# Rebuilding w_r and w_v in the score banks of the second batch's first head, with VectorE making the low halves

## The chip, the cores and the metric

The kernel runs on one core of a Trainium2 chip. The metric is the device time of one execution in microseconds (us). The core has five queues of work that matter here: TensorE (PE, the matmuls, with its weight loads PEld), VectorE (DVE), ScalarE (ACT), GpSimd (POOL) and SyncE (SP, which issues every DMA). PSUM is the accumulator memory that TensorE writes; SBUF is the working memory.

## What is computed

Two stages follow one another: an attention whose queries are pooled in pairs, and a channel mix ("ff" below) over the attention's output.

```python
q_pool = q.reshape(B, H, S // 2, 2, D).mean(axis=3)      # B 8, H 8, S 1152, D 64
scores = scale * q_pool @ k^T;  attn = softmax(scores);  x = attn @ v     # x: (8, 576, 512)
xk = mu_k * x + (1 - mu_k) * x_prev;  xr = mu_r * x + (1 - mu_r) * x_prev
k = relu(xk @ w_k)                 # w_k 512 x 1024
v = (k * k) @ w_v                  # w_v 1024 x 512
out = sigmoid(xr @ w_r) * v        # w_r 512 x 512
```

Inputs and output are float32. The kernel splits each float32 factor into a 16-bit high half and a 16-bit low half and adds three products (high by high, high by low, low by high). The weights are split once, at the start.

## The kernel before

**Attention.** The 64 heads (n = 0 to 63, eight to a batch) are worked on in turn, and each head's 576 pooled queries in six blocks of 96 (`block`). A block i has one of three score slots in PSUM, `s_b[i % 3]`, two banks wide. Its chain is: nine matmuls of scores (L530), the row maximum on VectorE (L537), a transpose of it (L540), a second maximum (L544), a matmul that spreads it (L546), a copy on ScalarE into the queries' low half (L550), nine more matmuls (L556), and the exponential on ScalarE (L562), which empties the slot. GpSimd makes the low half of the result (L565). `window` then multiplies with v (L591, L593, L598) into the bank `a_b`, and a head's result goes into `xt`, of which there are three, one for each batch in turn.

**Channel mix.** `ff` works on tiles of 256 rows of x. For each tile it mixes neighbouring rows (L734, L737, L743, L745), does the k product in four pairs of f through the PSUM bank `f_b` (matmuls L765; relu L792, square L794, low half L796), and then, for two halves of 128 rows, the r product, four ScalarE operations, a gate on VectorE (L820), the v product and a last VectorE product (L829). A tile becomes possible when its batch's attention is done; batch 0 holds tiles 0 and 1 whole. The tile loop stands at the end of each batch (L861 and after).

**Weights.** `weights` splits one block of 128 x 512 of a weight matrix at a time: w_k has 8 blocks, w_r 4 and w_v 8. The raw 64-bit pairs come by DMA (512 KB a block) into one of four staging buffers, `st[0]`, `st[1]` and two that lie in `xt[2]`. ScalarE turns the high words into `f_b` in PSUM (L680) and the top bytes in place (L684). VectorE joins both into `ex` in SBUF (L687, mode 'W1'). ScalarE writes the 16-bit high half (L697), and GpSimd subtracts it to give the low half (L702). All 20 blocks are placed beside the attention of batch 0, w_k first. One GpSimd memset (L844) then gives `xt[2]` back for batch 2.

**Order.** Every operation is put on a list with what it reads and writes (`Issue.add`). The order of issue on each of the five queues is a stored, compressed list (`TURNS`); engines issue in that order, and the dependences are kept by semaphores. While the order is laid out, `gaps` puts filler matmuls on zeros (L871) into TensorE's pauses of the first 150 us of its own planned time.

Of the kernel before, what the change touches and what calls it, by code (L numbers as in the profile page):

```python
# [12 lines left out]
F32 = mybir.dt.float32  # L13
# [6 lines left out]
ALU = mybir.AluOpType  # L20
# [30 lines left out]
    "c-n<}349e*miMW8Rqxf?>+Nfjm*i#N6S6_rx3C3}2!s|42!gVyAVdX31-DU*+S1zMzBS|Yw4<QyXe)F(-D=~~O4C7H={U9ss3^h@mplJ+E1>gz{r"  # L51
    "$dk->bTH_vQT0a;r$S>7-?Hh!l!bB4Z;}Rg>XhBpeFHqAHO;9`}d+L_WXQOD2)aYr1?cM4V(eoJ6`onwNCHk2Ewvq#2q=bJ$J0#~suh4$W?aOe3m"
    "!b-U)EsNH7hDL<*Y+oq|y8rMQ0P19qVrn+ouI2<Ln!*F;a4#lqMZi?6gcE3I1uxnZ*?1*TT@601j*EA!NMHSVE@I%rQ(fpc9N;ubHcpZ*7DhE(IW"
    "Ot<O_ITKZLd6ueId!|PC!8tLRGU*R$mhDgU<^-c+(%BA(;4$76HdiYVq`cCXUy=#?J<YlTSO5(pX?5g-5x_Fw^ooJvpdkVk96H;i+Q=Y;fciKhU!"
    "!8d3lC2L=J~L?9jb-okAH|H5IdCWwe4=hU=0ys@uq>dLp^GR&CVHSM8Bp!U}L*!mPtCtJkDGVMo6d&CAp6eqE3998i~QV)}8_p?d8U=9=URp&wmC"
    "MXZ~y5$`YdRBnz%HVvDcN+VE766vvmSS+3si{++9q|+%R+mgv-G#XFDYogJpZ6F~Wixq^!;oNWp!4^V0VUqE1ZOHEr_(5hQ;`dW9m>&#LFyJ-4UY"
    "|GO^@Y5Xy+}0!6fjNG?e@9d<i_8HrvRCT&oB%;Iow9TZ#c=}$LjdK<n>^=9GVUua@a{Pp#1!Te6r=)K$Of$CR1vHC_hX2nf!EKG8|4*2o#TnqEQN"
    "llax#(6BIX1J)-4>qrOns=kt+26!S&nQHn-9YDjgtOqa{!^|@Vcx9aqh&*x7oU~~^U)D7KXklpTbdo_>8>(LCCtIg$V)tpXE)9jv<$CK16HJ8gBa"
    "h14T0heJQo%zG<8XI%bXt0#SFvwvCr-KUZnfy$q8l%mqYObng)09dTq?Ek8++51Z$<0Zm6CjGm^WsG5N=i|Z64_)T9*<KDDXB;rD`skDG^#aGgV$"
    "!OBeS|w^_!TNN15n$Fp(V~bYqatjt(b=U>NO2d&6qOsM8!?4AA8=oJa)gG#bXa7&2Db?J~F^#+nZvve~i1Xvshzdz*d8e7jw>%Q+O}gS{Qoa`O<>"  # L60
    "9A+!5aVC+IYfGnd5HM!2OjM0TBWY60LkTLLOtE+@PFf@~GQv!vVYFIAYxIPu-aX4texFZOeIC{AaJjJBAmwbGTuu%~voXn-;4}tdn1F*e!jKa(ii"
    "}Gz{^fGPF(datBGL-Zq><B!IZWhfj6=H^t4*!0tgfoAvR76(=9JH>D6de<kX%d^w(|0d(lRP7Ei5c7D$EvTsj!TcOjAi|F)7(BRTYqyHzftiNwot"
    "afK`qyJ#5%QN<~wu8jsJ36DAo`6bds_0|=Tw6ozaIXeKkg2NVu@JONL=S!*s2n1Lm{m1a!lFfIZnbDvKIWK>TO)A1WL4i7%B$L&VDgAKpmi8*3!`"
    "C6_4e#y(3gfKx%BPo%{<Rx-)hURo5V_r^94%t$%WPS{k1DGdMNi~^J)mV(8!C*KTgltzL#OST73+o|mdN3IB1<=3l4ay-0%n>|nKabn%33|+Wb8W"
    "3mC;xK4iJ^vFAQQXi$NqUd5HR4jPA5>K>n?H{F^EtjG};I*I-jMf;q}U$$!4*@g@sNdKfj{@fabKE{QUgI`T3N|3|)}PP+p#zo109glSu$2oo3D="
# [222 lines left out]
def kernel(  # L288
# [221 lines left out]
    def block(n, j, i, t):  # L510
# [337 lines left out]
    for n in range(B * H):  # L848
# [63 lines left out]
```

## Time and profile before

| | |
|---|---|
| median of 3 runs | 1111.04 us (1110.21 to 1111.13) |
| the profiled execution, whole | 1111.68 us |
| its span, first to last instruction | 1109.9 us |
| TensorE busy | 1084.1 us (98%) |
| TensorE weight loads busy | 896.5 us (81%) |
| VectorE busy | 882.0 us (79%) |
| ScalarE busy | 842.0 us (76%) |
| GpSimd busy | 805.3 us (73%) |
| DMA moved | 135.38 MB |

The profile's page gives the busy time of each engine; the view by windows gives the same for any stretch; the view by groups gives the mean duration of each kind of instruction. A matmul's duration in these views is from its start to the end of its last result, and matmuls overlap in the array, so that a stretch can show TensorE "busy" though it does less than it could. How much it does is counted from the number of matmuls and the distance between their starts.

### The profile page before, as it was taken

Reading aid. Unit: us, or ns where it says so; the run is one execution under the profiler, and the core shown is the slowest. Engines: PE = TensorE matmul, PEld = TensorE weight load, DVE = VectorE, ACT = ScalarE, POOL = GpSimd, SP = SyncE. Lnnn points to the kernel's source line nnn. Section 1 sums busy time; section 2 is a strip of 40 time slices with the busy share of each in tenths; the row PEclk is TensorE's granted clock in tenths of the full one; section 3 lists DMA queues with packets and bytes.
Section 4 is the critical chain, followed back from the end, with each engine's and each line's share of the span. In section 5 each row is a group of like instructions: output and inputs, shape, how many; then the busy total and the mean of one; then the engine's idle time right before and its main releaser. Section 6 shows DMA issues by size and latency. Waiting matters only on the chain.

```text
span 1109.9 us, 45181 instructions
## 1 busy us (share of the span) xinstructions
PE 1084.1 (98%) x19046; PEld 896.5 (81%) x19046; DVE 882.0 (79%) x1587; ACT 842.0 (76%) x1804; POOL 805.3 (73%) x940
## 2 busy tenths in 40 slices
PE   7888999999999999999999999999999999999998
PEld 7777888988788897988797888888797979787564
DVE  7888888899898888888787888787888889773321
ACT  6899987877777786877877777878777778765643
POOL 4778978877768786878777786868688768755431
PEclk9999999999999999999999999999999999999999
DMA  9989557766567755656555565556556365420000
GB/s 246 220 220 221 136 123 147 144 152 108 135 125 133 148 108 104 142 131 129 135 94 128 122 126 113 124 135 110 128 111 150 83 129 100 88 40 23 19 20 29
DMA packets 258155, 135.38 MB, mean 122 GB/s; under 512 B 193440, under 2 KB 230304, under 8 KB 257952
## 3 DMA queue, kind: packets, MB, share of 16 engines
q1 hardware_dynamic: 257952, 132.50, 55.5%
q8 instruction: 149, 2.44, 0.9%
q14 instruction: 54, 0.44, 0.1%
HBM read 67.11 MB, written 9.44 MB: 69 GB/s over the span
## 4 chain that ended last, share of the span: by engine, by line
PE 70%; DVE 1%; issue 0%; ACT 0%; DVEq 0%
PE f L765 28%; PE s L556 9%; PE s L530 9%; PE a L591 5%; PE a L593 5%; PE a L598 4%; PE s L765 4%; PE a L765 2%; PE s L540 1%; PE s L546 1%; DVE mx L537 0%; DVE xr L737 0%; DVE xk L737 0%; DVE qn L435 0%; DVE mb L544 0%
## 5 line engine op out<-in xcount | busy, mean ns | idle before, releaser
L537 DVE TENSOR_REDUCE mx<-s 128x96 f16<-128x864 f32 x384 | 399.9, 1053 | 85.5 <-PE s L530 42.3
L565 POOL TENSOR_SCALAR pl<-pf 128x864 f16<-128x864 uint16 (+1 forms) x384 | 333.5, 869 | 143.6 <-ACT pf L562 108.9
L562 ACT ACTIVATE pf<-s 128x864 int32<-128x864 f32 x384 | 335.0, 885 | 89.6 <-PE s L556 64.8
L591 PE MATMUL a<-vt,pf 128*128 128x65 f16 x2880 | 238.7, 193 | 0.7 <-DVE xb L622 0.4
L593 PE MATMUL a<-vt,pf 128*128 128x64 f16 x2880 | 239.1, 193 | 0.0
L530 PE MATMUL s<-qT,ks 128*128 128x96 f16 x3456 | 221.4, 206 | 6.0 <-ACT pf L562 4.6
L556 PE MATMUL s<-qT,ks 128*128 128x96 f16 x3456 | 214.3, 206 | 4.2 <-ACT qT L550 3.9
L591 PEld LDWEIGHTS <-pf 128*128 128x128 f16 x2880 | 202.4, 98 | 5.1
L530 PEld LDWEIGHTS <-ks 128*128 128x128 f16 x3456 | 181.7, 98 | 29.1 <-issue 8.0
L593 PEld LDWEIGHTS <-pf 128*128 128x128 f16 x2880 | 193.1, 97 | 8.4 <-issue 1.2
L556 PEld LDWEIGHTS <-ks 128*128 128x128 f16 x3456 | 178.6, 98 | 24.3 <-issue 4.5
L550 ACT ACTIVATE qT<-s 1x96 f16<-1x96 f32 x384 | 88.2, 233 | 77.7 <-PE s L546 70.1
L544 DVE TENSOR_REDUCE mb<-s 128x1 f16<-128x128 f32 x384 | 108.9, 287 | 40.9 <-PE s L540 33.5
L765 PE MATMUL f<-xlk,wk_hi 128*128 128x256 f16 x496 | 135.2, 272 | 0.1
L765 PE MATMUL f<-xhk,wk_hi 128*128 128x256 f16 x496 | 135.1, 272 | 0.0
L765 PE MATMUL f<-xhk,wk_lo 128*128 128x256 f16 x496 | 135.2, 273 | 0.0
L598 PE MATMUL a<-vb,pl 128*128 128x65 f16 x2304 | 126.6, 193 | 0.4 <-POOL pl L565 0.2
L765 PEld LDWEIGHTS <-wk_hi 128*128 128x128 f16 x1152 | 105.6, 98 | 14.4
L598 PEld LDWEIGHTS <-pl 128*128 128x128 f16 x2304 | 101.0, 98 | 6.9 <-POOL pl L565 0.4
L796 POOL TENSOR_TENSOR gl<-g 128x512 f16<-128x512 f32 x72 | 76.9, 1069 | 40.5 <-ACT g L794 37.0
L478 POOL TENSOR_TENSOR kn<-kr,kn 128x320 f16<-128x320 f32 (+1 forms) x126 | 97.0, 784 | 6.0 <-ACT kn L473 1.8
L765 PE MATMUL f<-wv_lo,g 128*128 128x512 f16 x240 | 90.9, 379 | 0.0
(114 smaller groups left out, 2174.1 us busy)
## 6 DMA issues: line engine op xcount, KB each, us to landing
kr<-in_k_dram SPq DMA_DIRECT2D x64, 288.0 KB, 3.3
vr<-in_v_dram SPq DMA_DIRECT2D x64, 288.0 KB, 3.3
qr<-in_q_dram SPq DMA_DIRECT2D x32, 320.0 KB, 3.6
ks<-ks SPq DMA_DIRECT2D x64, 144.0 KB, 2.7
out_dram<-em SPq DMA_DIRECT2D x36, 256.0 KB, 2.3
qr<-in_q_dram SPq DMA_DIRECT2D x32, 256.0 KB, 3.3
st<-in_moe_w_k_dram SPq DMA_DIRECT2D x4, 512.0 KB, 5.5
xt<-in_moe_w_k_dram SPq DMA_DIRECT2D x4, 512.0 KB, 6.5
```

The source lines that it names most:

```text
L478: lambda cs=cs, en=nc.vector if ve else nc.gpsimd: en.tensor_tensor(kn[i][:, cs, D:P], kr[i][:, cs], kn[i][:, cs, 0:D], op=ALU.subtract),
L530: nc.tensor.matmul(cols(c, c + 1), ks1[hp][:, c, :], qhi, start=(c == c0), stop=False, skip_group_check=True)
L537: op("DVE", 0.974, lambda: nc.vector.tensor_reduce(mxz[:, P - QN:P], grid(0, NC).rearrange("p c q -> p q c"), axis=AX.X, op=ALU.max), r=[( ...
L544: op("DVE", 0.199, lambda: nc.vector.tensor_reduce(mbz, s[:, 0:P], axis=AX.X, op=ALU.max), r=[("s", z)], w=[("mb", z)], key=t + O_MAX)
L550: op("ACT", 0.15, lambda: nc.scalar.activation(qlo[0:1], s[0:1, 0:QN], AF.Prelu, scale=1.0 - EPS, alpha=(1.0 + EPS) / (1.0 - EPS)), r=[("s ...
L556: nc.tensor.matmul(cols(c, c + 1), ks2[hp][:, c, :], qlo, start=False, stop=True, skip_group_check=True)
L562: op("ACT", NC * QN / 1200 + 0.051, lambda: nc.scalar.activation(pf[:, :, HALF + rows.start:HALF + rows.stop], grid(0, NC), AF.Exp, bias=S ...
L565: op("POOL", 0.93 if buf == ("pside",) else NC * (r1 - r0) / 1200 + 0.273, lambda: nc.gpsimd.tensor_scalar(to, half(pf, U16, 0)[:, :, HALF ...
L591: nc.tensor.matmul(a_b[:, a0:a0 + VN], half(pf, F16, 1)[:, c, his], vt[jv][:, c, D:D + VN], start=(w == 0 and c == 0), stop=False, skip_gr ...
L593: nc.tensor.matmul(a_b[:, a0:a0 + D], half(pf, F16, 1)[:, c, his], vt[jv][:, c, 0:D], start=False, stop=(side and c == NC - 1), skip_group ...
L598: nc.tensor.matmul(a_b[:, a0:a0 + VN], pl[:, c, rows], vb[jv][:, c, 0:VN], start=False, stop=(c == NC - 1), skip_group_check=True)
L765: nc.tensor.matmul(ps, terms[i][0], terms[i][1], start=(first and i == 0), stop=(i == last), skip_group_check=True)
```

## The change

Four things change.

1. Mode 'W3' takes the place of 'W1' for all weights: VectorE joins the two parts in place in PSUM, ScalarE copies the high half out of PSUM, and VectorE (not GpSimd) subtracts it there to give the low half. `ex` is no longer used by the weights; the PSUM place is held from the first ScalarE operation to the last subtraction.
2. The 12 blocks of w_r and w_v leave batch 0. They are rebuilt in head 8, the first of batch 1, two blocks ahead of each of its six score blocks, each in one bank of the slot that this score block takes next. Their first operation waits for the slot to be empty, and the score block's first matmul waits for both.
3. The second half of the first ff tile (r and v products, `gates`) is put off until head 8's last score block; the second tile of batch 0 and the memset of `xt[2]` follow it.
4. The stored order of issue is a new one.

```diff
         for c0, c1 in BK:
             op("PE", (c1 - c0) * 0.0425, lambda c0=c0, c1=c1: scores(c0, c1),
-               r=[("ks1", hp, c) for c in (0, 5) if c < c1 and (c0 < 5 or c)] + kh, w=[("s", z)], key=t)
+               r=[("ks1", hp, c) for c in (0, 5) if c < c1 and (c0 < 5 or c)] + kh, w=[("s", z), ("su", z, 0), ("su", z, 1)], key=t)
...
-    def weights(n, w, kc, key, step):
+    def weights(n, w, kc, key, step, slot=None):
...
-                u, kf = f_b, ("f",)
+                u, kf, free = f_b, ("f",), []
+                if slot:
+                    z, o = slot[0] % 3, slot[1]
+                    u, kf, free = s_b[z][:, o * 512:(o + 1) * 512], ("su", z, o), [("s", z)]
+                    key = slot[2]
                 ui = u.bitcast(I32)
                 op("ACT", 0.52, lambda u=u, wh=wh: nc.scalar.activation(
-                    u, wh.bitcast(F32), AF.Prelu, scale=2.0 ** -111, alpha=-2.0 ** 32), r=[ks], w=[kf], key=key)
-                mode = {'k': 'W1', 'r': 'W1', 'v': 'W1'}[n]
+                    u, wh.bitcast(F32), AF.Prelu, scale=2.0 ** -111, alpha=-2.0 ** 32), r=[ks], w=[kf] + free, key=key)
+                mode = {'k': 'W3', 'r': 'W3', 'v': 'W3'}[n]
...
                 key += step
+                yield
...
-        for s0 in range(0, n, P):
...
+        def gates(key_):
+            nonlocal key
+            key = key_
+            for s0 in range(0, n, P):
...
+            return key
+
+        if t0 == 0:
+            rest.append(gates)
+            return key
+        return gates(key)
...
-    weights("k", w_k, NG, W_FIRST * PER, W_STEP * PER)
-    weights("r", w_r, NG, W_REST * PER, W_REST_STEP * PER)
-    weights("v", w_v, NF, (W_REST + 4 * W_REST_STEP) * PER, W_REST_STEP * PER)
-    op("POOL", 0.2, lambda: nc.gpsimd.memset(xt[2][:, :, 0:1], 0.0), w=[(m, j) for m in ("st", "sl") for j in (2, 3)] +
-       [("xt", 2, g, k0) for g in range(NG) for k0, k1 in TURN], key=W_REST * PER + 14 * W_REST_STEP * PER)
+    early = list(weights("k", w_k, NG, W_FIRST * PER, W_STEP * PER))
+    slot = [0, 0, 0.0]
+    later = iter([*[(weights, "r", w_r, NG)], (weights, "v", w_v, NF)])
+
+    def rebuilt():
+        for f_, *w in later:
+            yield from f_(*w, 0.0, 0.0, slot)
+
+    more = rebuilt()
+    rest = []
...
         for j in range(NB):
             i = n * NB + j
+            if n >= H and rest:
+                for o in range(2):
+                    slot[:] = i, o, i * PER
+                    next(more, None)
             block(n, j, i, i * PER)
...
+            if n >= H and rest and j == NB - 1:
+                fkey = rest.pop()((i + 1) * PER)
+                while tiles and tiles[0][1] <= b * TQ:
+                    fkey = ff(*tiles.pop(0), fkey, False)
+                op("POOL", 0.2, lambda: nc.gpsimd.memset(xt[2][:, :, 0:1], 0.0), w=[(m, j) for m in ("st", "sl") for j in (2, 3)] +
+                   [("xt", 2, g, k0) for g in range(NG) for k0, k1 in TURN], key=i * PER)
         if h == H - 1:
             fkey = max(fkey, (n + 1) * NB * PER)
-            while tiles and tiles[0][1] <= (b + 1) * TQ:
+            while tiles and tiles[0][1] <= (b + 1) * TQ and not rest:
                 fkey = ff(*tiles.pop(0), fkey, b == B - 1)
```

The body of `gates` is the old loop, indented. The changed strings of `TURNS` are left out. In mode 'W3', which stood in the kernel but wasn't used, the two VectorE operations of a block are:

```python
e, ke = u, kf
v_(0.6, lambda ui=ui, wl=wl: nc.vector.scalar_tensor_tensor(
    ui, ui, 3, wl, op0=ALU.logical_shift_left, op1=ALU.bitwise_or), [kl, kf], [kf])
...
v_(0.6, lambda lo=lo, e=e, hi=hi: nc.vector.tensor_tensor(lo, e, hi, op=ALU.subtract),
   [ke, ("w", n, c, f)], [("wl", n, c, f)])
```

More of the change, by code (lines that the diff above doesn't have):

```diff
@@ L56 @@
[L56 to L65, printed above, removed]
@@ new lines @@
+    "<t(SDiX_>a6ekEp^I9Hc}K{P$G{{mdNHI*(W<>hf7sea+2b(D~3b2D+<cVb}}TJT_f^IvMP~_;woujnZlA?qC_MmktBsBiF7BCL`o#0DK5p6r8-o"
+    "f8q>+{w<$K#{0gc|CKN|Vk!8iMDgh;;$RtaSU?k|!9GVf99FpBm5!I>2yk6CzsEQILd%*9stCXcEs5dH}4WTMS2`Nz-y>Nx_un~4hs$@Ou^QvJ*S"
+    "5YPqpdde+tthFOqNx0A1o<9rIVMvq?9`o3XH+sY$>FA`7S#Nj7SU8)ji^y_1svp1)s!Ap6@J{Ig>gmhNZgJQMaj^dnr6hqS`<@f<mB+BpTaJOUA0"
+    "q4$N1H(n4UmSTuNS^>cG=@*lx4g+!W5v)|?(q3v05+A@db!4hP0UTsp|l>Zzp4z11l<f*S2;P?2q6*$7+h#<dWhC5gxH2$LAGXcQ?@Y?w(|ma!mK"
+    "uoLodjzke7MA;M!A;uHIXgrD#i`pWQKp+$d1cCvZztqMB^CJ--Ldu4vC$GorA-6wBD52}f))5SH8BSa|bF;mK0y8`qltB&$X4dQUkylmSx=~@cQP"
@@ new lines @@
+    "5@A?RL9^RO>3D*qp_f3>!}uBh5ihRm0e(Ynm*pvLx9Q48fy%Itazx?H-q%N21McP*rUvX?9h$OPZ>vcA!GG$u{6HOOmCeoWQ7~6p2wNQlo`~p^6|"
+    "SNG6(ynKuG~4%zRMy&jM3_PCvH0}ybM<dzJ><#Le@7;9R7o~9`ZuZ6DnwCTD_pWLYHn$xK%9tUpd`Y62>xyVttoZaA}(I}TBr$e(jFfh=7oK9Jbj"
+    "M2tmU_c2Fh&7Z8)V$o>+`L>hN6toGGMP$JB0Dde^W>a(oMN#=GC}cpEEdhmCQ2rgMDc<&#V8u}BVY{_zc&_-*<(@AN8t%VD3@KuI@)*Y`FWDWGd+"
+    "f^A)(_uwG*_AM*(*fbhB00n-N`lo{llN89lfN>x?c9E12uS7+f}+bNsl7j^%V{q{?=Tz?PQf{F*%OEO!?JkP9$^{3PYd+1WXWlodmWlN60+M<b~e"
+    "l_jM_p`3^(uqaVLEC4)unTJt#fP4YU_%nVP@bNIFAS{>-<W^HgqMb;08OUwaCZZEQ(N*-n-G$Dg|ApK&#jA-?RqC7@)OoCmgBOZdpofc)HqpnhQf"
@@ L140 @@
+    "r#*%SGK%BEg@{h?>LsdEszbDSu)ar8qKzAu3GsrZb7Hax8V8&zFOQ<iWZdysIhpvYbvgxLR8)J}oe?>UOec>{WI<7CMjTp-Sct>uiaHjgm62W^pl"
+    "zwdBd=c}DXw!ZiEQn3R``IrfHl|J3dEW|Jr7k$9iY(44w6?u@ZuF!*x}P0Li{%-<C$RIOBkZ#?NFr7*Sec)VDaqv-?&6DcW<@DN3NqHSK(h!pVo{"
+    "g`#}9f-&6_M;USSe!~4KHjy}1e6@AYFOVI2{f^!0K33chr@9?;{XEwrspKf?5B8%!~X>s&{$9"
 )
@@ L798, in ff @@
                r=[("g", f0)], w=[("gl", f0)], key=key + 1)
-        for s0 in range(0, n, P):
-            ss = slice(s0, s0 + P)
-            ps, pk = f_psum(tail)
-            terms = []
-            for c in range(NG):
-                r = xkeys("r", c) + wk("r", c, 0)
-                terms += [(hr[:, c, ss], whi["r"][:, c, :], r), (hr[:, c, ss], wlo["r"][:, c, :], r),
-                          (xl["r"][:, c, ss], whi["r"][:, c, :], r)]
-            products(ps[:, 0:DM], pk, terms, DM / 2400.0 + 0.0025, 1)
-            z = turn("ex")
-            e, m_ = ex[z], em[z]
-            ps_r = ps[:, 0:DM]
-            ke, km = ("ex", z), ("em", z)
-            op("ACT", 0.48, lambda e=e, ps=ps_r: nc.scalar.activation(e, ps, AF.Abs, scale=0.5 / (SV * SW)),
-               r=[pk], w=[ke], key=key + O_DONE)
-            op("ACT", 0.48, lambda m_=m_, ps=ps_r: nc.scalar.activation(m_, ps, AF.Relu, scale=-1.0 / (SV * SW)),
-               r=[pk], w=[km], key=key + O_DONE)
-            op("ACT", 0.52, lambda e=e: nc.scalar.activation(e, e, AF.Tanh), r=[ke], w=[ke], key=key + O_DONE)
-            op("ACT", 0.52, lambda m_=m_: nc.scalar.activation(m_, m_, AF.Exp, scale=-1.0), r=[km], w=[km],
-               key=key + O_DONE)
-            op("DVE", 0.602, lambda e=e, m_=m_: nc.vector.scalar_tensor_tensor(
-                e, e, 1.0, m_, op0=ALU.add, op1=ALU.mult), r=[ke, km], w=[ke], key=key + O_GATE, port=True)
-            ps, pk = f_psum(tail)
-            terms = []
-            for f in range(NF):
-                r = [("g", f // 2 * 2), ("gl", f // 2 * 2)] + wk("v", f, 0)
-                terms += [(gh[:, f, ss], whi["v"][:, f, :], r), (gh[:, f, ss], wlo["v"][:, f, :], r),
-                          (gl[:, f, ss], whi["v"][:, f, :], r)]
-            products(ps[:, 0:DM], pk, terms, DM / 2400.0 + 0.0025, 1)
-            op("DVE", 0.605, lambda e=e, m_=m_, ps=ps[:, 0:DM]: nc.vector.scalar_tensor_tensor(
-                m_, ps, 0.5 / (SV * SV * SW), e, op0=ALU.mult, op1=ALU.mult),
-               r=[pk, ke], w=[km], key=key + O_DONE)
-            op("DMA", 0.7, lambda m_=m_, t=t0 + s0: nc.sync.dma_start(out_f[t:t + P], m_), r=[km], key=key)
@@ L833, in ff @@
-        return key
+        def gates(key_):
+            nonlocal key
+            key = key_
+            for s0 in range(0, n, P):
+                ss = slice(s0, s0 + P)
+                ps, pk = f_psum(tail)
+                terms = []
+                for c in range(NG):
+                    r = xkeys("r", c) + wk("r", c, 0)
+                    terms += [(hr[:, c, ss], whi["r"][:, c, :], r), (hr[:, c, ss], wlo["r"][:, c, :], r),
+                              (xl["r"][:, c, ss], whi["r"][:, c, :], r)]
+                products(ps[:, 0:DM], pk, terms, DM / 2400.0 + 0.0025, 1)
+                z = turn("ex")
+                e, m_ = ex[z], em[z]
+                ps_r = ps[:, 0:DM]
+                ke, km = ("ex", z), ("em", z)
+                op("ACT", 0.48, lambda e=e, ps=ps_r: nc.scalar.activation(e, ps, AF.Abs, scale=0.5 / (SV * SW)),
+                   r=[pk], w=[ke], key=key + O_DONE)
+                op("ACT", 0.48, lambda m_=m_, ps=ps_r: nc.scalar.activation(m_, ps, AF.Relu, scale=-1.0 / (SV * SW)),
+                   r=[pk], w=[km], key=key + O_DONE)
+                op("ACT", 0.52, lambda e=e: nc.scalar.activation(e, e, AF.Tanh), r=[ke], w=[ke], key=key + O_DONE)
+                op("ACT", 0.52, lambda m_=m_: nc.scalar.activation(m_, m_, AF.Exp, scale=-1.0), r=[km], w=[km],
+                   key=key + O_DONE)
+                op("DVE", 0.602, lambda e=e, m_=m_: nc.vector.scalar_tensor_tensor(
+                    e, e, 1.0, m_, op0=ALU.add, op1=ALU.mult), r=[ke, km], w=[ke], key=key + O_GATE, port=True)
+                ps, pk = f_psum(tail)
+                terms = []
+                for f in range(NF):
+                    r = [("g", f // 2 * 2), ("gl", f // 2 * 2)] + wk("v", f, 0)
+                    terms += [(gh[:, f, ss], whi["v"][:, f, :], r), (gh[:, f, ss], wlo["v"][:, f, :], r),
+                              (gl[:, f, ss], whi["v"][:, f, :], r)]
+                products(ps[:, 0:DM], pk, terms, DM / 2400.0 + 0.0025, 1)
+                op("DVE", 0.605, lambda e=e, m_=m_, ps=ps[:, 0:DM]: nc.vector.scalar_tensor_tensor(
+                    m_, ps, 0.5 / (SV * SV * SW), e, op0=ALU.mult, op1=ALU.mult),
+                   r=[pk, ke], w=[km], key=key + O_DONE)
+                op("DMA", 0.7, lambda m_=m_, t=t0 + s0: nc.sync.dma_start(out_f[t:t + P], m_), r=[km], key=key)
+            return key
```

155 lines of the change are left out of this document (76 added, 79 removed).

## The prediction

> **What bounds the kernel now.** I began with the view by windows of the whole trace, cut where its character changes (us, then busy time and number of instructions of PE, PEld, DVE, ACT, POOL, then the granted clock, DMA share and GB/s).
>
> ```profile
> 0.00:20.00 20.00, 15.38 (x240) 14.18 (x240) 14.26 (x40) 11.70 (x25) 9.07 (x19) 0.91 0.97 234
> 20.00:120.00 100.00, 86.70 (x1974) 78.59 (x1972) 87.64 (x167) 91.99 (x193) 78.64 (x89) 1.00 0.96 224
> 120.00:150.00 30.00, 27.98 (x517) 24.92 (x514) 25.08 (x46) 25.47 (x59) 26.13 (x32) 1.00 0.51 124
> 150.00:950.00 800.00, 797.93 (x14540) 669.05 (x14538) 686.12 (x1212) 624.09 (x1350) 618.53 (x715) 1.00 0.59 124
> ```
>
> From 150 to 950 us TensorE is busy for 797.93 of 800 us, and every other engine has slack: VectorE 14%, ScalarE 22%. Before 120 us it is the other way: ScalarE, at 92%, is the fullest engine, VectorE follows at 88%. The page's chain of waits says the same of the whole:
>
> ```profile
> PE 70%; DVE 1%; issue 0%; ACT 0%; DVEq 0%
> ```
>
> So the end is set by TensorE's work plus the time that it lost before it became full. I count that loss. The view by groups, of TensorE's matmuls in the first 150 us:
>
> ```profile
> L530 PE MATMUL s<-qT,ks 128*128 128x96 f16 x549 | 34.7, 207 | 6.0 <-ACT pf L562 4.6 <-ACT qT L452 1.1
> L593 PE MATMUL a<-vt,pf 128*128 128x64 f16 x423 | 33.3, 193 | 0.0
> L591 PE MATMUL a<-vt,pf 128*128 128x65 f16 x423 | 33.3, 193 | 0.6 <-ACT xt L650 0.2 <-DVE xb L622 0.2
> L556 PE MATMUL s<-qT,ks 128*128 128x96 f16 x531 | 32.1, 208 | 3.5 <-ACT qT L550 3.2
> L598 PE MATMUL a<-vb,pl 128*128 128x65 f16 x324 | 16.5, 193 | 0.1
> L871 PE MATMUL s<-zero 128*128 128x128 f16 x174 | 14.7, 224 | 0.0
> L540 PE MATMUL s<-identb,mx 128*128 128x128 f16 x60 | 13.1, 222 | 3.2 <-DVE mx L537 2.9
> L546 PE MATMUL s<-negi,mb 128*128 128x96 f16 x60 | 12.6, 211 | 4.5 <-DVE mb L544 4.4
> L765 PE MATMUL f<-xhk,wk_hi 128*128 128x256 f16 x25 | 6.8, 272 | 0.0
> ```
>
> Their means of 193 to 272 ns overlap, so they aren't summed. The chain in order of time (start, length, what) gives the step from one to the next:
>
> ```profile
> 483.84 0.77 PE s L556 x18
> ...
> 1026.35 5.18 PE f L765 x24
> ```
>
> That is 0.043 us for 96 columns and 0.216 us for 512. Scaled by columns (an estimate) it is 0.029 for 64 or 65, 0.057 for 128 and 0.108 for 256. The work done by 150 us is 1080 x 0.043 + (846 + 324) x 0.029 + 60 x 0.057 + 60 x 0.043 + 74 x 0.108 = 94 us, with the transposes 95 (the 174 fillers on zeros don't count). **TensorE has lost 55 us by then, and the change can only alter this number**, as long as TensorE stays full afterwards.
>
> **Batch 0.** One score block costs TensorE 18 x 0.043 + 0.057 + 0.043 us of scores and a sixth of its head's 126 products with v (126 x 0.029 = 3.7): 1.48 us, so 48 blocks need 71 us. The exponential's row for the first 120 us shows when they are through:
>
> ```profile
> L562 ACT ACTIVATE pf<-s x48: 863/886/894, 14.0 to 118.2; 128x864 int32<-128x864 f32 x48
> ```
>
> 48 blocks by 119 us. What fills ScalarE and VectorE beside them, in the groups of 20 to 120 us:
>
> ```profile
> L684 ACT ACTIVATE xt<-xt 128x512 int32<-128x512 uint8 x10 | 6.8, 677 | 0.0
> L680 ACT ACTIVATE f<-xt 128x512 f32<-128x512 f32 x10 | 6.3, 630 | 0.0
> L684 ACT ACTIVATE st<-st 128x512 int32<-128x512 uint8 x9 | 6.0, 672 | 0.0
> L680 ACT ACTIVATE f<-st 128x512 f32<-128x512 f32 x9 | 5.7, 632 | 0.0
> ...
> L697 ACT CAST wk_hi<-ex 128x512 f16<-128x512 f32 x8 | 4.9, 608 | 0.0
> ...
> L697 ACT CAST wv_hi<-ex 128x512 f16<-128x512 f32 x5 | 3.0, 605 | 0.0
> L697 ACT CAST wr_hi<-ex 128x512 f16<-128x512 f32 x4 | 2.4, 601 | 0.0
> ```
> ```profile
> L687 DVE SCALAR_TENSOR_TENSOR ex<-f,xt 128x512 int32<-128x512 int32 x9 | 6.2, 684 | 1.0 <-ACT f L680 0.8 <-issue 0.2
> L687 DVE SCALAR_TENSOR_TENSOR ex<-f,st 128x512 int32<-128x512 int32 x9 | 6.1, 682 | 1.0 <-POOL wv_lo L702 0.6 <-issue 0.4
> ```
>
> Weights hold ScalarE for 35.1 of its 92 us. Eight blocks of each kind are w_k's and stay; w_r and w_v have 11 x 0.675 + 11 x 0.63 + 9 x 0.605 = 19.8 us here. **Removed:** ScalarE falls to 72 us. VectorE loses 10 x 0.683 = 6.8 us. **Added:** 8 subtractions for w_k. No row shows this form; the nearest on VectorE reads PSUM and SBUF over the same 512 columns, and the upper end is what GpSimd took:
>
> ```profile
> L829 DVE SCALAR_TENSOR_TENSOR em<-f,ex 128x512 f32<-128x512 f32 x30 | 20.6, 687 | 8.0 <-PE f L765 7.7
> ```
> ```profile
> L702 POOL TENSOR_TENSOR wv_lo<-ex,wv_hi 128x512 f16<-128x512 f32 x8 | 9.8, 1220 | 0.4
> ```
>
> I take 0.69 us, 5.5 us in all (upper end 9.8). VectorE then has 86.3 us in this stretch and becomes the bound. If it stays 88% full, batch 0 gains 1 to 2 us; if it reaches 97%, which no engine does in this stretch, 11 us. I take 92%, what ScalarE reached as the fullest: 94 us, so batch 0 is through at 113 us, **6 us earlier**. GpSimd's 23 us of subtractions go too; it wasn't the fullest, so that is worth nothing beyond the waits of VectorE on it (0.6 us above). w_k's blocks hold `f_b` for four operations instead of two; nothing else uses it before ff, so that is free.
>
> **Head 8.** Now 12 blocks stand beside six score blocks. ScalarE: 12 x (0.675 + 0.63 + 0.605) = 22.9 us, less 2.7 for the four top-byte passes whose buffers can be loaded early, is 20.2. A score block costs ScalarE (92 - 35.1 - 2) / 44 = 1.25 us; the last two blocks of w_v are ahead of block 53 and need only the slots of blocks 45 to 50, so five blocks, 6.3 us, lie between. The first ff tile's k part belongs here as well:
>
> ```profile
> L794 ACT ACTIVATE g<-r 128x512 f32<-128x512 f32 x72 | 45.0, 627 | 1.7
> L734 ACT ACTIVATE tmp<-xt,omu_k 128x256 f32<-128x256 f32 (+3 forms) x96 | 42.0, 446 | 12.3 <-POOL xt L636 4.1 <-DVE xr L737 3.9 <-DVE xk L737 3.8
> L792 ACT ACTIVATE r<-f 128x512 f32<-128x512 f32 x62 | 36.7, 592 | 11.6 <-PE f L765 10.8
> ...
> L743 ACT CAST xhk<-xk 128x256 f16<-128x256 f32 x72 | 27.7, 395 | 3.6 <-PE s L765 1.4 <-DVE xk L737 1.3 <-PE a L765 0.5
> ```
>
> Four of each: 8.2 us. Sum 34.7 us, some 37 at 95%, counted from block 45's exponential (about 109 us): **all weights are there at 146 us**. VectorE has 12 x 1.37 = 16.4 us for the weights and 1.65 us a block, less than ScalarE. By 146 us TensorE can have done batch 0 (71), three and parts of three more blocks of head 8 (6.5), the k part of tile 0 (96 x 0.108 = 10.4), one r product (12 x 0.216 = 2.6) and v terms as far as `f_b` and w_v allow (5): 95.5. Lost: 50.5 us instead of 55. From there two tiles' rest and head 8 fill TensorE.
>
> **The sum** is -4.5 to -5 us. Against the profiled execution (1111.68, its span 1109.9) that gives 1107; that execution lies 0.6 above the median of the runs, so I predict **1106.3** for the median.
>
> **Waits added.** The first rebuilding operation waits for the exponential of the slot's last block, which stands ahead on ScalarE's own queue: free. The new wait that counts is on TensorE: the scores of blocks 48 to 53 wait for VectorE's last subtraction, and behind them in order stand products with v and ff. **DMA.** Twelve loads of 512 KB move; four can still be early. SP issues in order, and a load waits for its buffer; behind it stand the next heads' k, v and transposes.
>
> ```profile
> st<-in_moe_w_v_dram SPq DMA_DIRECT2D x4, 512.0 KB, 4.3
> ```
>
> Four buffers serve two score blocks, so a round may take about 12 us at 6 us a block; 4.3 us of landing, 1 to 2 of issue and 2 of work fit. Cover gone (landing over 8 us): a stall of 2 to 4 us.
>
> **A rule against it.** The granted clock is 0.91 in the first 20 us and 1.00 after. The Trainium skill, "TensorE: Matmul & The Clock Gate", Part 1, says that after an idle window of about 3.4 us TensorE's clock falls to half for at least as long. Should the rebuilding leave such a gap, that would cost 1.7 us (an estimate from that page), and the sum would be 1108; the trace shows the low clock only at the start, and no run here shows it at such a place.
>
> **Rivals.**
> (1) *The gain is given back* (0.24): VectorE stays at 88% and is the bound through batch 1, since it takes on 20 x 0.69 us.
>
> ```profile
> L562 ACT ACTIVATE pf<-s x97: 863/891/909, 14.0 to 246.0; 128x864 int32<-128x864 f32 x97
> ```
>
> Batch 1's attention ends at 245 us, just as the ff of two tiles (52 us) runs out; later, and TensorE waits. For it: 88% is what is shown. Against: VectorE has 14% free afterwards. Batch 0 ends 1 to 2 us earlier only, weights come at 150 us: 1109 to 1112.
> (2) *Slower* (0.20): TensorE stalls at the scores of head 8, behind the slots. A slot turned over in 3 x 100 / 45 = 6.7 us; with two rebuilt blocks (0.63 + 0.63 + 0.68 + 0.6 + 0.69 = 3.2) it is 9.9: 3.3 us a block with three slots overlapped, 9.9 with none. My sum has 6.1. The break-even is 55 us lost, weights at 150.5, 6.8 us a block; at 8 us a block the weights come at 157: +7, 1118. For it: the order on each queue is fixed, and it can't be read from the diff. Against: ff and blocks of other slots can stand between.
> (3) *More* (0.14): VectorE reaches 97%, batch 0 ends at 108 and the rebuilding keeps its 37 us: 141, loss 45 to 46: 1100 to 1101.
> (4) *It doesn't do what it says*: the low halves or the move alone decide nothing because TensorE finds ff work either way. That is (1)'s time.
>
> **How the numbers follow.** The forecast (1103 to 1109) has 0.42. The range to hold 8 in 10 runs from 1096 (rival 3, with the 5% that I leave ScalarE idle in head 8 and some of tile 0's 8.2 us taken out too) to 1118 (rival 2 at its price). A measurement here tells 0.2% (2.2 us) from no change: faster, below 1108.8, takes most of the forecast and rival 3: 0.54. Same: 0.25, of which most is rival 1. Slower, above 1113.3: 0.21.
>
> **What would show it.** In the profile after: 48 exponentials by about 113 us; ScalarE in batch 0 near 80%, VectorE above it; the twelve rebuilt blocks between 109 and 146 us; TensorE full from there; its matmuls by 150 us worth 99 to 100 us instead of 95. Wrong if batch 0 still ends near 119, if head 8's blocks are over 6.8 us apart, or if TensorE has gaps after 150 us.

## The result: slower, 1118.58 us

| | before | after |
|---|---|---|
| median | 1111.09 us (4 runs, 1110.21 to 1111.73) | 1118.58 us (4 runs, 1118.47 to 1118.82) |
| the profiled execution, whole | 1111.68 us | 1118.82 us |
| its span | 1109.9 us | 1117.0 us |

The ratio is 1.0068, 95% interval 1.0055 to 1.0081: the change costs 7.5 us. The prediction was a gain of 5 us, and its range ended just short, at 1118.

The view by windows of after, cut where the one of before was cut (columns as there: PE, PEld, DVE, ACT, POOL busy and their instructions, granted clock, DMA share, GB/s):

```profile
20.00:120.00 100.00, 87.82 (x1996) 79.69 (x1994) 91.80 (x178) 87.40 (x187) 63.98 (x79) 1.00 0.90 217
120.00:150.00 30.00, 25.93 (x375) 22.03 (x376) 27.29 (x47) 28.13 (x59) 13.93 (x19) 0.94 0.64 159
150.00:950.00 800.00, 794.77 (x14545) 666.81 (x14544) 676.25 (x1202) 616.81 (x1339) 612.96 (x711) 1.00 0.58 123
```

Three things can be read from it. In batch 0 the roles changed as forecast: VectorE is the fullest at 91.80%; ScalarE fell from 92% to 87%, though not to the 80% forecast. From 120 to 150 us TensorE runs 375 matmuls where before ran 517 (before's were in larger part the short ones of attention, so the count alone overstates the loss), at a mean clock of 0.94, while ScalarE is 94% full. And from 150 to 950 us TensorE is idle for 5.2 us instead of 2.1. That last row is the one to stop at: the changed work is over by then.

The chain of waits over the whole of after gives the same picture: VectorE's and ScalarE's shares, 1% and 0% before, have grown.

```profile
PE 82%; DVE 5%; ACT 3%; issue 1%; DVEq 0%; ACTq 0%
```

**Counting the lost time.** Busy shares hide most of the loss, since matmuls overlap. So I counted for both traces as the prediction did: up to a time t, each matmul by its columns (0.0025 us + columns/2400, which gives the prediction's 0.043 us for 96 columns), fillers not at all; t less that sum is what TensorE has lost. The float32 transposes count as twice their columns, since in the trace they follow one another at 0.11 us. The counts include all transposes, which the prediction put at 1 us and which are some 3 us; so they stand lower than its 55.

| lost by TensorE (us), up to | 100 | 115 | 120 | 146 | 160 | 200 | 300 | 600 | 1090 |
|---|---|---|---|---|---|---|---|---|---|
| before | 40.2 | 44.8 | 45.9 | 52.7 | 52.8 | 53.1 | 54.9 | 60.7 | 65.6 |
| after | 36.7 | 41.8 | 45.1 | 54.0 | 53.9 | 54.4 | 58.7 | 67.0 | 72.8 |
| difference | -3.5 | -3.0 | -0.8 | +1.3 | +1.1 | +1.3 | +3.8 | +6.3 | +7.2 |

The 7.2 us at the end agree with the spans (7.1). After is ahead until 115 us, has given that back by 146, and then loses another 6 us with no weights left to rebuild. Two stretches put the later part beside each other; the windows of before:

```profile
200.00:300.00 100.00, 99.69 (x1833) 83.46 (x1830) 88.61 (x158) 78.79 (x173) 79.04 (x92) 1.00 0.67 141
300.00:1090.00 790.00, 788.24 (x13534) 646.87 (x13533) 618.65 (x1101) 586.37 (x1257) 568.26 (x660) 1.00 0.50 106
```

and of after:

```profile
200.00:300.00 100.00, 98.26 (x1924) 83.89 (x1921) 86.41 (x155) 79.27 (x172) 79.59 (x93) 1.00 0.56 121
300.00:1090.00 790.00, 785.93 (x13491) 643.29 (x13489) 617.31 (x1106) 582.22 (x1258) 570.03 (x661) 1.00 0.51 107
```

TensorE is idle for 1.4 and 2.3 us more. The remaining 2.2 us of the 5.9 lost in these two stretches stand as later starts within time that the view calls busy.

**The start, in after's own rows.** The exponentials by 120 us, and VectorE's subtractions for the 12 moved blocks, from the views by line (count, shortest, median and longest in ns, start of the first and last):

```profile
L562 ACT ACTIVATE pf<-s x48: 863/891/897, 13.9 to 114.9; 128x864 int32<-128x864 f32 x48
```
```profile
L703 DVE TENSOR_TENSOR wv_lo<-s,wv_hi x8: 677/681/693, 125.0 to 144.9; 128x512 f16<-128x512 f32 x8
L703 DVE TENSOR_TENSOR wr_lo<-s,wr_hi x4: 681/684/685, 113.8 to 121.3; 128x512 f16<-128x512 f32 x4
```

Batch 0 is through at 115.8 us (3 us earlier, not 6). The last weights are there at 144.9 + 0.7 = 145.6 us; the prediction had 146. So the rebuilding took place when it was meant to. TensorE's products in the first 150 us, from the view by groups:

```profile
L770 PE MATMUL f<-xhk,wk_hi 128*128 128x256 f16 x32 | 8.7, 272 | 1.9 <-ACT r L797 1.9
...
L770 PE MATMUL f<-wr_hi,xr 128*128 128x512 f16 x3 | 1.1, 379 | 0.0
L770 PE MATMUL f<-wr_lo,xr 128*128 128x512 f16 x2 | 0.8, 379 | 0.0
L770 PE MATMUL f<-wr_hi,xlr 128*128 128x512 f16 x2 | 0.8, 379 | 0.0
```

All 96 matmuls of the first tile's k part, seven of the r product, none with w_v. The k part waits for ScalarE's relu (L797), which empties `f_b`, and ScalarE has the rebuilding to do. Of the 40 us from 106 to 146 the chain in order of time spends 18.0 on VectorE, 17.1 on ScalarE and 0.5 on TensorE. A cut from it (start, length, what; the shortest pieces left out):

```profile
119.25 0.54 ACT st L688
120.10 0.50 ACT s L684
120.65 0.42 ACT xt L650
121.08 0.52 ACT s L684
121.60 0.43 ACT tmp L739
122.03 0.57 ACT xt L688
```

In that pause the clock gave way, as windows of 2 us show (by the granted clock in them, half speed lasted 3.4 us, from 121.4 to 124.8):

```profile
120.00:122.00 2.00, 1.39 (x11) 1.04 (x12) 2.00 (x5) 2.00 (x6) 0.00 (x0) 0.85 0.95 303
122.00:124.00 2.00, 1.44 (x19) 1.30 (x17) 1.97 (x6) 2.00 (x7) 0.08 (x1) 0.50 1.92 188
124.00:126.00 2.00, 2.00 (x27) 1.89 (x25) 2.00 (x4) 2.00 (x5) 1.75 (x3) 0.80 0.61 121
```

### The profile page after: what moved, and what is told of

It reads as the page before. It is cut to its first block, busy times and chain, and to the rows that moved or that the text cites. A ratio compares the mean times of both kernels' runs of the same rounds, so it can differ in the third digit from the quotient of the medians.

```text
span 1117.0 us, 45180 instructions
## 1 busy us (share of the span) xinstructions
PE 1087.1 (97%) x19066; PEld 898.1 (80%) x19066; DVE 885.3 (79%) x1607; ACT 839.4 (75%) x1804; POOL 780.8 (70%) x920
## 4 chain that ended last, share of the span: by engine, by line
PE 82%; DVE 5%; ACT 3%; issue 1%; DVEq 0%; ACTq 0%
PE f L770 34%; PE s L530 11%; PE s L556 11%; PE a L591 6%; PE a L593 6%; PE a L598 5%; PE s L770 4%; DVE mx L537 2%; PE a L770 2%; PE s L540 2%; PE s L546 1%; ACT pf L562 1%; DVE vt L500 1%; DVE mb L544 0%; DVE s L699 0%
## 5 line engine op out<-in xcount | busy, mean ns | idle before, releaser
L770 PE MATMUL f<-xhk,wk_hi 128*128 128x256 f16 x496 | 135.1, 272 | 3.4 <-ACT r L797 2.9
L770 PE MATMUL f<-xhk,wk_lo 128*128 128x256 f16 x496 | 135.2, 273 | 0.0
L770 PE MATMUL f<-xlk,wk_hi 128*128 128x256 f16 x496 | 135.1, 272 | 0.0
L598 PE MATMUL a<-vb,pl 128*128 128x65 f16 x2304 | 129.0, 193 | 1.1 <-issue 1.0
L770 PEld LDWEIGHTS <-wk_hi 128*128 128x128 f16 x1152 | 106.4, 98 | 18.9 <-issue 4.1
L478 POOL TENSOR_TENSOR kn<-kr,kn 128x256 f16<-128x256 f32 (+1 forms) x126 | 95.9, 770 | 13.4 <-ACT kn L473 7.6
L770 PE MATMUL f<-wv_hi,g 128*128 128x512 f16 x240 | 90.9, 379 | 0.5 <-ACT em L823 0.5
```

The costliest lines, as they stand in the source:

```text
L478: lambda cs=cs, en=nc.vector if ve else nc.gpsimd: en.tensor_tensor(kn[i][:, cs, D:P], kr[i][:, cs], kn[i][:, cs, 0:D], op=ALU.subtract),
L598: nc.tensor.matmul(a_b[:, a0:a0 + VN], pl[:, c, rows], vb[jv][:, c, 0:VN], start=False, stop=(c == NC - 1), skip_group_check=True)
L770: nc.tensor.matmul(ps, terms[i][0], terms[i][1], start=(first and i == 0), stop=(i == last), skip_group_check=True)
```

## The experiments

My theory after the result: two separate costs. The first: between 106 and 146 us ScalarE and VectorE are the bound, and TensorE finds less to do there than I had counted. The second: the new stored order of issue, which came with the change, loses some 6 us after 200 us wherever it is used. The rival to the second: the later loss follows from the late weights (work pushed back, buffers out of step), and the order is innocent. (In what was expected of E1, E2 and E6, theory A is the order and theory B its rival.)

The stored order covers every instruction, so a kernel with another program needs an order of its own. Where an experiment says "order of before from 215 us", the operations planned after that time on the one side follow in the sequence of the other, and those before it keep theirs; a join of the two, a seam, is at 215 to 300 us.

### E1, E2: exchange the later order alone

E1 is the program of after with the order of before from 215 us on; E2 is the program of before, weights and all, with the order of after from 215 us on. The edit is in the strings of `TURNS` alone:

```diff
 TURNS = (
-...
+...
 )
```

> The changed kernel, with its own order of issue for everything that its plan starts before 215 us and the old kernel's order for all that comes later. Of the 7.5 us that the change cost, the count of TensorE's work puts 1.3 us before 200 us and about 5 between 200 and 700. Theory A (the later part of the new stored order is simply worse): 1112.5 to 1114.5, and TensorE's loss after 200 us falls to that of before. Theory B (VectorE, with 20 subtractions more, runs the attention late, so that TensorE has gaps whatever the later order): 1117 to 1119.

> The old kernel, its weights beside batch 0 as ever, with the new kernel's order of issue for all that is planned after 215 us. Theory A: 1115 to 1117, 5 us slower than the old kernel without any of the change to the weights. Theory B: 1110 to 1112.

Measured: E1 1117.1 us (1116.22 to 1117.98), ratio 1.0057 [1.0044, 1.0070]; E2 1117.34 us (1116.05 to 1118.67; theory A had 1115 to 1117), ratio 1.0059 [1.0046, 1.0071]. E2 has the weights of before, and until 240 us it runs as before does (52.2 us lost by 160, before 52.8). Yet it is as slow as E1. Its loss from 200 to 300 us is 4.4 (before 1.8, after 4.3) and from 300 to 1090 us 14.4 (before 10.7, after 14.1). The windows of E2:

```profile
300.00:1090.00 790.00, 785.75 (x13496) 643.81 (x13495) 617.74 (x1106) 582.12 (x1258) 568.48 (x660) 1.00 0.50 107
```

and of E1:

```profile
300.00:1090.00 790.00, 787.67 (x13540) 645.67 (x13539) 621.99 (x1106) 586.44 (x1258) 572.98 (x663) 1.00 0.50 107
```

TensorE's busy time there goes with the order (785.75 and 785.93; 787.67 and 788.24), not with the program. The waits of TensorE and its weight loads from 300 to 1000 us (engine and line, what it waited for, us in all, times, longest) are even the same ones. After:

```profile
PE f L770 <- ACT r L797: 1.0, 2, 0.7
...
PEld L540 <- DVE mx L537: 1.9, 8, 0.5
PEld L770 <- issue: 1.6, 3, 0.8
```

E2 (its own line numbers: L761 is after's L770, L536 its L540):

```profile
PE f L761 <- ACT r L788: 1.0, 2, 0.7
...
PEld L536 <- DVE mx L533: 1.9, 8, 0.5
...
PEld L761 <- issue: 1.6, 3, 0.8
```

Before has no wait for relu and half as many for the first maximum; its largest group are five for the second:

```profile
PEld L546 <- DVE mb L544: 2.0, 5, 0.6
PEld L540 <- DVE mx L537: 1.1, 4, 0.5
```

So the late weights aren't needed for the loss: with the later order, a program whose weights weren't touched is about 6 us slower. From 300 us on, past the seam, that shows the second cost (3.7 us more than before), and there the rival falls. The 2.6 us more between 200 and 300 us contain E2's seam, so they show less. E1 alone would have misled, since its time is the one of theory B. It gained only 1.5 us on after, because its own start was worse (54.7 us lost by 160 us, the clock at half for 6.8 us) and it lost at the seam: 3.7 us between 200 and 240, where after loses 1.1. From 300 us on it loses 11.4, close to before's 10.7.

### E6: the same exchange with the seam at 280 us

The edit is again in `TURNS` alone, as above.

> The changed kernel with its own order up to 280 us of its plan and the old kernel's after that. Theory A (each later order loses its own amount, here 10.7 us instead of 14.1 from 300 us to the end): 1114.5 to 1116, with the waits of the old kernel after 300 us. Theory B (the late losses belong to the program, not to the order): 1118 to 1119.

Measured: 1118.34 us (1117.59 to 1119.5), ratio 1.0066 [1.0053, 1.0078]. The time is the one of theory B. The loss and the waits after 300 us are those of theory A: it loses 10.7 from 300 to 1090 us, exactly as before, and the longest waits of its weight loads from 300 to 1000 us are before's (L541 and L535 here are before's L546 and L540):

```profile
300.00:1090.00 790.00, 788.27 (x13544) 645.99 (x13543) 623.24 (x1108) 586.94 (x1262) 572.03 (x664) 1.00 0.50 108
```
```profile
PEld L541 <- DVE mb L539: 2.0, 5, 0.6
PEld L535 <- DVE mx L532: 1.1, 4, 0.5
```

From 280 to 300 us, at the seam, it loses 2.8, where after loses nothing, and that takes back most of the gain. The order's cost from 300 us on is confirmed. What after would take with before's later order and no such seam isn't: I have no version of that.

### E3, E10: the move, with the low halves on GpSimd

E3 keeps after's program but for the mode:

```diff
-                mode = {'k': 'W3', 'r': 'W3', 'v': 'W3'}[n]
+                mode = {'k': 'W1', 'r': 'W1', 'v': 'W1'}[n]
```

> The changed kernel with the low halves made by GpSimd from SBUF again (mode W1); w_r and w_v still in the score slots of head 8, the order otherwise the changed kernel's. If VectorE's 12 subtractions (8 us) in head 8 are what the rebuilding stretch waits for, TensorE's loss up to 150 us falls by 2 to 4 us and the time is 1114 to 1116. If ScalarE and the slots set it, or GpSimd's longer subtraction is now late itself, 1117 to 1120.

Measured: 1137.68 us, ratio 1.0242 [1.0228, 1.0256]. Most of that is no property of the mode: the order that I had made for E3 was also disturbed after 215 us, and the loss there is 30 us from 200 to 1090. Only its first 160 us can be read: 57.2 us lost, with the clock never at half in that stretch. E10 is the same program with the order of before from 215 us on, undisturbed, to be compared with E1.

> Program of E1 (after's program, from 215 us on the order of before), but with mode W1 for all weights: VectorE joins into ex in SBUF, the low halves are made by GpSimd; w_r and w_v stay in the slots of head 8. It is E3 without the scrambled order after 215 us. If VectorE's 20 subtractions (0.68 us each) are what eats the gain of batch 0, TensorE has lost 1 to 2 us less by 160 us than E1 (54.7), and the time is 1115 to 1116. If the rebuilding in head 8 is a chain that waits for its slowest step, GpSimd's 1.22 us in place of 0.69 a block lengthens it: loss by 160 us 56 to 57 (E3 had 57.2), the time 1118 to 1120.

Measured: 1120.04 us (1118.85 to 1120.67), ratio 1.0077 [1.0064, 1.0091], 3 us above E1. By 160 us it has lost 57.8 (E1 54.7, after 53.9). Its exponentials and GpSimd's subtractions:

```profile
L557 ACT ACTIVATE pf<-s x48: 863/886/897, 13.6 to 117.8; 128x864 int32<-128x864 f32 x48
```
```profile
L701 POOL TENSOR_TENSOR wv_lo<-ex,wv_hi 128x512 f16<-128x512 f32 x8 | 9.7, 1227 | 2.8 <-ACT wv_hi L696 2.7
```

The second branch of its expectation held, and a little more than that. In after's early order the program with GpSimd's 1.2 us instead of 0.68 in the chain of a block loses 3 us more of TensorE, and batch 0 is through at 118.7 instead of 115.8 (E1 116.6). The clock isn't the reason alone: E10 has it at half for 10.2 us and E1 for 6.8, but E3 lost nearly as much as E10 with no half clock. So in this place VectorE did better with the low halves, and they are not what ate the gain. (E10 also kept after's plan of starts, made for the other mode; how far an order of its own would help wasn't tried.)

### E4, E8: VectorE's low halves, without the move

E4 is before with mode W3 for all 20 blocks, all of them in `f_b` during batch 0; E8 has it for w_k's eight alone, and exactly before's order from 215 us on. Up to there each has an order of its own, which the moved subtractions need.

```diff
-                mode = {'k': 'W1', 'r': 'W1', 'v': 'W1'}[n]
+                mode = {'k': 'W3', 'r': 'W3', 'v': 'W3'}[n]      # E4
+                mode = {'k': 'W3', 'r': 'W1', 'v': 'W1'}[n]      # E8
```

> The old kernel with the low halves of all 20 weight blocks made by VectorE out of PSUM (mode W3), everything where it was. It puts 13.7 us on VectorE, which is 88% full in batch 0, and takes 24 us from GpSimd. If VectorE and the single bank f_b, now held twice as long, bind there: 1114 to 1118. If ScalarE alone is the bound: 1110 to 1112.

> The old kernel with the low halves of w_k alone made by VectorE out of PSUM (8 subtractions, 5.5 us more on VectorE, 9.4 us less on GpSimd), the order from 215 us on exactly the old one's. If VectorE binds in batch 0, as the run with all 20 blocks suggests (2.4 us more lost by 120 us): 1 to 3 us slower, 1112 to 1114. If it was the bank f_b held longer just before ff that cost there, w_k is far from ff and nothing changes: 1110 to 1112.

Measured: E4, whose order after 215 us differs a little from before's, 1120.61 us, ratio 1.0091 [1.0078, 1.0105], 58.3 us lost by 160; E8 1115.52 us (1115.29 to 1117.06), ratio 1.0044 [1.0030, 1.0057], 55.2 lost by 160 (before 52.8). Both are slower than either branch of what was expected. With eight subtractions, VectorE goes from 88% to 91.33% in batch 0, and TensorE loses 2.4 us more:

```profile
20.00:120.00 100.00, 86.37 (x1929) 77.58 (x1926) 91.33 (x168) 88.73 (x188) 66.65 (x79) 1.00 0.93 216
```

A part of that may be a wait that the prediction had called free, from the waits of ScalarE in E8 (L676 is the first operation of the next block of weights):

```profile
ACT f L676 <- DVE wk_lo L695: 2.0, 3, 0.9
```

Without the move, w_r's and w_v's blocks follow w_k's through the one bank `f_b` and wait for its last subtraction. In after, where they have other banks, this wait isn't among ScalarE's in batch 0. In the orders that were run, each part of the change alone is slower than before, as both together are. How much of E8's 2.4 us is VectorE's share, how much this wait and how much the new early order can't be told from it. E8 also shows that a join of orders isn't costly in itself: between 200 and 300 us it loses 2.0, before 1.8, and from 300 us on 10.7 as before.

### E5: more fillers in the pause

The clock fell for 3.4 us, so E5 gives `gaps` more fillers. That should keep the clock up and change nothing else in the work (the dip began at 121.4 us, not at 121.7 as the expectation has it):

```diff
-share=0.6, dense=0.62
+share=0.8, dense=0.9
```

> The changed kernel with more filler matmuls on zeros in TensorE's pauses of the first 150 us (share 0.8 for 0.6, dense 0.9 for 0.62). In the changed kernel TensorE ran at half clock for 3.4 us from 121.7 us, in the middle of the rebuilding. If that dip costs work: no dip here, and 1 to 1.7 us faster, 1116.9 to 1117.6. If TensorE had nothing to do there anyway, or the fillers get in the way of real matmuls: 1118 to 1120.

Measured: 1121.57 us (1121.35 to 1122.55), ratio 1.0095 [1.0081, 1.0109]: 3 us slower than after, and beyond both branches. The window of the pause in the profiled execution:

```profile
120.00:150.00 30.00, 25.79 (x400) 22.23 (x401) 27.15 (x48) 28.09 (x59) 13.07 (x19) 1.00 0.63 171
```

The clock is 1.00 throughout here, yet 55.8 us are lost by 160, after 53.9. The edit adds fillers alone (400 in 150 us instead of 264), so they cost this; that they stand ahead of real matmuls in the queue is my reading of it and not shown. Only this one of E5's four runs has a mean clock of 1.0: it took 1121.35 us, and the three others, at 0.998, took 1121.4 to 1122.55. The runs of before made beside E5 hint at what a dip costs: four at a mean clock of 0.998 took 1111.5 to 1112.1 us, ten at 0.999 or 1.0 took 1109.7 to 1111.1. The medians are 1.3 us apart; whether that is the dip or the pause that brought it can't be told from them.

### E7, E9: the weights for nothing

How much could the rebuilding be worth at all? E7 is after without loading and rebuilding w_r and w_v:

```diff
     def rebuilt():
-        for f_, *w in later:
-            yield from f_(*w, 0.0, 0.0, slot)
+        yield from ()
+
+    for n_, kc in (("r", NG), ("v", NF)):
+        for c in range(kc):
+            for d_, m_ in ((whi, "w"), (wlo, "wl")):
+                op("POOL", 0.45, lambda t_=d_[n_][:, c]: nc.gpsimd.memset(t_, 0.0), w=[(m_, n_, c, 0)], key=-1.0)
```

> The changed kernel without w_r and w_v: their 12 blocks are neither loaded nor rebuilt, GpSimd fills them with zeros in 24 memsets spread over batch 0, so the r and v products are of zeros; the order otherwise the changed kernel's. It is the most that any place for the rebuilding could give with this order. If the rebuilding stretch (115 to 146 us) is bound by the rebuilding on ScalarE and VectorE, TensorE's loss by 160 us falls from 53.9 to 45 to 49 us, and the time is 1110 to 1114: the later order still takes its part. If the fixed order holds TensorE back there: 1116 to 1119.

Measured: 1110.85 us (11 runs), ratio 1.0000 [0.9991, 1.0009]. Its loss by 160 us is 45.6, 8.3 less than after and 7.2 less than before. Batch 0 is through at 113.5:

```profile
L557 ACT ACTIVATE pf<-s x48: 863/890/897, 14.0 to 112.6; 128x864 int32<-128x864 f32 x48
```

And it isn't faster than before. From 300 to 1090 us it loses 14.6, as after and E2 do: the later order gives back everything that twelve blocks of weights for nothing bring. E9 settles this. It is E7 with the order of before from 215 us on; its edit beside E7 is in `TURNS` alone.

> Program of E7 (blocks of w_r and w_v neither loaded nor rebuilt, their halves set to zero; the r and v products multiply zeros), but from 215 us on with the order of issue of before, as in E1. Theory (the later order costs by itself, whatever happens with the weights): E7 lost 50.9 us by 300 us and 65.5 by 1090 (14.6 between); with the order of before the stretch 300 to 1090 us loses 10.7 to 11.4, so 1107 us, less what the seam at 215 to 300 us costs (up to 2.5): 1106.5 to 1109.5, faster than before by 0.2 to 0.4%. Rival (the loss of the later order hangs on the weights' work that ran ahead of it, or my E7 was not slow for that reason): no change against E7, 1110.9.

Measured: 1107.93 us (1107.18 to 1108.54), ratio 0.9973 [0.9962, 0.9983]. The loss from 300 to 1090 us falls from 14.6 to 10.7, between 200 and 300 us it stays at 4.7 (E7 4.6), with the seam in it. TensorE's row of E7,

```profile
300.00:1090.00 790.00, 785.77 (x13448) 644.00 (x13446) 613.98 (x1094) 579.78 (x1252) 565.82 (x657) 1.00 0.51 106
```

becomes in E9

```profile
300.00:1090.00 790.00, 788.27 (x13502) 646.64 (x13500) 616.11 (x1097) 582.81 (x1251) 566.40 (x656) 1.00 0.50 106
```

So from 300 us on the later order's cost appears with before's weights (E2, 3.7 us), with after's (after against E6, 3.4) and with none (E7 against E9, 3.9). Between 200 and 300 us it isn't separated: every program with the moved weights, or without them, loses 4.3 us or more there, under either order, and only E8 comes as low as before's 1.8. None of the complete kernels that I ran is faster than before; E9 leaves work out, and so shows only where a ceiling lies for this early order: about 3 us below before with a seam, perhaps 6 if the seam could be avoided, which no run shows (an estimate: 2.9 us of E9's 4.7 between 200 and 300 are more than before's 1.8).

## Why the prediction was wrong, step by step

**What bounds the kernel: right.** The end moved by what TensorE lost: 7.2 us counted, 7.1 in the spans.

**Batch 0: mechanism right, size half.** VectorE did become the bound, at 91.80% against the 92% taken, and the join and the subtraction cost 0.70 and 0.68 us (0.68 and 0.69 taken). But the 48 blocks are through at 115.8 and not 113. The term that was mis-sized is VectorE's work: I took 86.3 us for batch 0 and forgot that the rebuilding of w_r starts inside it and is served by the same two engines. By 115.8 VectorE has been busy for 88.1 us of the 95.8 since 20, again 92%. In E7, without that rebuilding, batch 0 ends at 113.5. ScalarE didn't fall to 72 us: it worked for 83.3 in those 95.8. The step "`f_b` is held for four operations, that is free" holds in after; by E8's wait it doesn't hold without the move.

**Head 8: the time of the weights right.** 145.6 us against 146, and after the 48th exponential six more follow by 146.6 us, 5.1 us apart on the mean of the starts (114.9 to 145.7), where the sum had 6.1. ScalarE's and VectorE's waits from 110 to 150 us name no DMA, so the loads that moved held up neither of them.

**TensorE's work by 146 us: the first step that failed.** I had put down 95.5 us of work, and with it a loss that falls by 4.5; measured, it rises by 1.3, a difference of 5.8 us. I summed what could be ready (k part, an r product, 5 us of v terms) as if ScalarE's 37 us of rebuilding and the emptying of `f_b` didn't compete. In the trace the k part alone holds `f_b` to 147.6 us, because each turn waits for a relu on ScalarE, at 94% the fullest engine of that stretch, with VectorE at 91%. By 146 us the count has 79.2 us of attention (77.5 put down) and 9.8 of the k part (10.4), but nothing of the r product (2.6) and nothing of the v terms (5). Of the r product's 12 matmuls 7 ran by 150 us, of the v terms none, and attention had one block of head 8 every 5 us. E7 shows the size. Without the rebuilding the count by 146 us has 83.5 of attention, 10.5 of k, 2.6 of r and 1.1 of v, so that the 5 for v was too high in any case. ScalarE is 75% full in this stretch, TensorE runs 454 matmuls instead of 375, and the loss by 160 us is 8.3 smaller (1.4 of it by 115 us):

```profile
120.00:150.00 30.00, 29.51 (x454) 24.53 (x453) 20.86 (x38) 22.50 (x47) 19.83 (x26) 1.00 0.33 81
```

**The clock: the dip named against the change came, but not by the rule.** In after the clock is at half for 3.4 us from 121.4, inside the pause. The Trainium skill, "TensorE: Matmul & The Clock Gate", Part 1, has the clock at half for at least about 3.4 us after an idle window. The trace agrees with the length and not with the condition: in the 3.4 us before the dip TensorE was idle for 1.6 us in all, 0.87 at the longest, and ran 18 matmuls. A thinly filled pause was enough here. The 1.7 us that I had estimated is not separated by the runs of after, which all have a mean clock of 0.997 or 0.998; E5 paid more for its fillers than it got.

**"As long as TensorE stays full afterwards": the second step that failed, and as large as the first.** I made that the condition of the sum and gave it no price, though the fourth part of the change says that the whole stored order is new; gaps after 150 us were the prediction's own sign of being wrong. Measured: 2.5 us more lost between 200 and 300 us and 3.4 between 300 and 1090, 5.9 in all. E2 shows that such a loss needs neither the move nor the low halves. For the 3.4 the cause is the later order; for the 2.5 it stays open between the order and what the moved work leaves behind. Together 5.8 + 5.9 = 11.7 us; the gap between forecast and median is 12.3.

**The rivals.** The second rival's time, 1118, came out, but not its mechanism: it asked for blocks over 6.8 us apart and weights at 157 us; they are 5.1 apart and there at 145.6. One turn of a slot was long (9.7 us between the 48th and 49th exponential, its 9.9 with nothing overlapped), and that is the pause in which the clock fell. The new wait that the prediction feared, TensorE's scores behind a subtraction, was 0.4 us from 106 to 150. That the time of this rival came out is luck. The first rival (gain given back by a full VectorE) is close to what happened until 200 us, through ScalarE and VectorE together. Why the new order is worse after 215 us, I can say only as far as the rows go: from 300 to 1000 us eight short waits of weight loads for the first maximum and two of matmuls for a relu, none over 0.7 us, and later starts in between. Which sequence in it causes them stays open.

One correction to the introduction: the three weight matrices come as 64-bit floats; that is why a block of 128 x 512 is 512 KB.

## What to carry to other kernels

A change that comes with a new static order of issue is two changes: price the order over the whole run, not only around the edit, and test it by running the old program in the new order. When work is moved off a full engine to a place where a second engine is to be fed, count what the first engine can deliver there, not what would be ready. And before tuning a move, run it with the moved work left out: here that showed a ceiling of a few us.

## What the runs showed of the hardware that was not expected

An order of issue alone, with the program left alone, moved the time by 6 us of 1111 (E2), through waits of under a microsecond each and later starts, on a TensorE that the view by windows calls over 99% busy. The clock fell to half for 3.4 us after a stretch in which TensorE was never idle for more than 0.87 us (after, 118.0 to 121.4). And more fillers, meant to hold the clock, cost 3 us more than letting it fall (E5 1121.57, after 1118.58).
